# Low parts of the first expert's first layer made on DVE instead of POOL at the end of the attention

## The chip, the cores and the metric

The kernel runs on one core of a Trainium2 chip. The metric is the time of one execution on the device in microseconds (us). Five engines work in parallel, each through its own instructions in the order in which they were written: PE (matrix products), DVE (elementwise work and reductions), ACT (activations, copies, casts), POOL (a second, elementwise engine, which also issues gathers and scatters) and SP (issues most DMA transfers). They meet at semaphores: an instruction that needs a result of another engine waits at the head of its queue, and what is queued behind it waits too.

## The reference

Three stages follow one another on 4 x 544 tokens of width 512, all in float32.

```
# 1. attention: 8 heads of 64; 32 global and 512 local tokens, window 32
out_g = sm(scale * q_g @ k_all^T) @ v_all          # global tokens see all
s_ll  = where(|i - j| <= 32, scale * q_l @ k_l^T, -1e9)
out_l = sm(concat(scale * q_l @ k_g^T, s_ll)) @ concat(v_g, v_l)
# 2. mixture of experts: 8 experts, 512 -> 1024 -> 512
e = argmax(x @ w_gate), or the expert of the token before it where the local gate holds
x = softmax(x @ w_gate)[e] * (relu(x @ w1[e]) @ w2[e])
# 3. gated layer: 512 -> 1024, convolution over 3 tokens, sigmoid gate, 1024 -> 512
h = relu(x @ w_in);  out = (h * sigmoid(conv3(h))) @ w_out
```

## The kernel before

**Attention.** The work of a batch is cut into 8 units, and 32 units (n = 0 to 31) run one after the other in one loop that is written out as a software pipeline. Two units with the same 128 tokens (n even: heads 0 to 3, n odd: heads 4 to 7) share one output tile. For a unit, PE writes the scores `sp` (L259, L267, both units of a pair at once), DVE takes the row extremes `nm` (L275), ACT makes the exponentials `pr` (L278, four instructions), PE transposes them (`ptp`, L286), ACT copies them out (`pts`, L288), and two rounds later PE multiplies by V (`op`, L300). When both units of a pair are through, DVE normalises the tile (`rc`, `rr`, then `x`, L307 to L311). There is one PSUM buffer for `op`, so the first `op` of the next pair waits until `x` of the pair before has been read. SP stores `x` to `x_dram`; PE transposes it (`trx`, L319), DVE copies it out (`xt`, L321), and four such tiles give the router's logits (`lgp`, L334; `L`, L349).

**Routing and experts.** Tokens are sorted into slots of 128 of one expert each. The matrices of an expert are needed as a high and a low part, since each float32 product is made as three passes (high by high, high by low, low by high). `split_k` makes one piece: ACT casts the weights `ws` to the high part `wh` (L1026), then an elementwise engine subtracts, `wl = ws - wh` (L1027). For the first layer a piece is 128x1024, and there are four (k = 0 to 3).

**The end of the attention.** The first two slots are routed early, so that their expert's weights can be loaded and split while the attention still runs. `hook(n, 1)` is called at the end of round n: in rounds 28 to 31 it splits one piece of the first layer each (`SPLIT_W1`), and in rounds 30 and 31 it issues the loads of the second layer, which overwrite `ws` once the pieces there have been split. After the last round the rest of the pipeline is drained by hand: `op` of unit 30 and `x` of the last pair, the first matrix products of the expert (`hp`, L1090) between them, the second layer's splits on DVE (`SPLIT_W2`), the logits, and then the full routing (`phase_b`), whose DVE chain begins at `L` (L349) while PE goes on with slots 0 and 1 between its steps. Where it is said below that a row belongs to unit n, it is by this order.

Of the kernel before, what the change touches and what calls it, by code (L numbers as in the profile page):

```python
# [1566 lines left out]
def moe_kernel(ctx, tc, q_l, k_l, v_l, q_g, k_g, v_g, w_gate, w_local, w1, w2, w_in, conv_w, w_out, out):  # L1567
    nc = tc.nc
    outf = out.rearrange("b s d -> (b s) d")
    with tc.manual_schedule():  # L1570
# [37 lines left out]
        def hook(n, end):  # L1608
            if n + end > 20 and (end or todo.get("y") != "pe"):
                for _ in range(STEPS_A[end]):  # L1610
                    todo["y"] = next(ph, 0)
                    if todo["y"] == "es":
                        todo["load"] = True
                    if todo["y"] in (0, "pe"):
                        break
            if not end:
                return
            if n == N_Y:
                nc.sync.dma_start(y_dram[0:S, :], x_dram[0:S, :])
            if n == 25:  # L1620
                right.close()
                hl = ctx.enter_context(tc.tile_pool(name="w_hl", bufs=1, side="right"))
                st = moe_ctx.enter_context(tc.tile_pool(name="w_x", bufs=1, side="right"))
                W = Weights(nc, hl, st)
                m = todo["m"] = Moe(warm, tc, W, ident, x_dram, y_dram, rt, w1, w2, w_in.bitcast(I32),
                                    w_out.bitcast(I32))
            m = todo.get("m")
            if todo.pop("load", False):
                W = m.W
                todo["e0"] = m.reg(nc.sync, 0, 0, E - 1)  # L1630
                for a in (0, 2):
                    W.load_k(1, w1[bass.ds(todo["e0"], 1)], a, a + 2)
            if m and todo.get("y") == 0 and not m.xs and not m.xt:
                todo["g"] = n
                ca.close()
                todo["xp"] = xa.enter_context(tc.tile_pool(name="m_xa", bufs=1, side="right"))
                for s in range(NA):
                    m.xs[s] = m.gather(s, todo["xp"])
            if n - todo.get("g", n) == GATHER_T:
                m.hs0 = todo["xp"].tile([P, FF], F32, name="hs0")  # L1640
                m.xt[0] = m.hi_lo_t(m.xs.pop(0), NKC, "x", todo["xp"], at.ps)
            for k in SPLIT_W1.get(n, ()):
                m.W.split_k(1, m.W.s, k, nc.gpsimd)
            if n in (30, 31):
                for a in range(2):
                    k = 4 * (n - 30) + 2 * a
                    m.W.load_k(2, w2[bass.ds(todo["e0"], 1)], k, k + 2)
            if n == 32:
                cs.close()
                m.psh = moe_ctx.enter_context(tc.tile_pool(name="m_h", bufs=1, space=PSUM, side="right"))  # L1650
                todo["fill"] = m.fill()
            if n >= 32:
                for _ in range(TAIL[n - 32]):
                    next(todo["fill"])
                for k in SPLIT_W2.get(n, ()):
                    m.W.split_k(2, m.W.s, k, nc.vector)

        at = Attn(at_ctx, right, cs, tc, q_l, k_l, v_l, q_g, k_g, v_g, wcat, wz, ident, x_dram, L, late(), hook)
        at.run()
        at_ctx.close()  # L1660
        m, W, fill = todo["m"], todo["m"].W, todo["fill"]
# [61 lines left out]
```

## Time and profile before

| what | value |
|---|---|
| median of 3 runs | 648.47 us (646.09 to 649.37) |
| profiled execution | 645.35 us, of which 643.6 us are its span |
| PE busy | 604.7 us, 94% of the span |
| DVE busy | 418.8 us, 65% |
| ACT busy | 320.9 us, 50% |
| POOL busy | 174.7 us, 27% |

The span runs from the first to the last instruction, and all times of rows count from its start. Busy shares are means over stages of different kinds: in the attention all engines take turns in one pipeline, in the experts and the gated layer PE has nearly no gap.

### The profile page before, as it was taken

The page shows a single profiled execution, that of the slowest core. Times are in us where ns is not written, and L with a number is a line of the kernel's source. Part 1 is how long each engine was busy: PE and PEld are TensorE (multiplying, and loading weights), DVE is VectorE, ACT ScalarE, POOL GpSimd, SP SyncE. Part 2 cuts the span into 40 slices and gives each one's busy share as a digit, 9 for nine tenths or more (in the row PEclk, how much of TensorE's full clock was granted, in tenths as well). Part 3 has the DMA queues.
Part 4 walks back from the last instruction along what each step waited for, and adds up shares of the span by engine and source line. Part 5 has one row for each costly group of instructions (what it writes and reads, how often), then busy time and mean ns, then how long its engine had stood idle before and what let it go on. Part 6 is the DMA issues. An engine that isn't in the chain of part 4 may idle for free. (4 is left out here: it accounts for less than half of the span.)

```text
span 643.6 us, 15270 instructions
## 1 busy us (share of the span) xinstructions
PE 604.7 (94%) x5898; PEld 508.0 (79%) x5898; DVE 418.8 (65%) x874; ACT 320.9 (50%) x629; POOL 174.7 (27%) x226
## 2 busy tenths in 40 slices
PE   8888898888999999999999999987999999999997
PEld 7666676665778888888888888857998898898986
DVE  7877577958836676875778677586893393393340
ACT  4754555573225546352454634664874374373331
POOL 7664810070212232423222251000042042300200
PEclk9999999999999999999999999997999999999999
DMA  9999668652158454953545494023101201000001
GB/s 226 217 244 236 177 142 209 240 168 75 55 201 314 140 182 171 344 207 132 211 143 184 145 347 157 16 86 88 31 20 49 68 16 50 34 1 34 34 34 49
DMA packets 60089, 88.12 MB, mean 137 GB/s; under 512 B 25710, under 2 KB 34182, under 8 KB 59976
## 3 DMA queue, kind: packets, MB, share of 16 engines
q1 hardware_dynamic: 56488, 76.83, 38.3%
q0 software_dynamic: 3520, 10.23, 4.6%
q8 instruction: 48, 0.79, 0.5%
q14 instruction: 33, 0.27, 0.1%
HBM read 125.87 MB, written 15.79 MB: 220 GB/s over the span
## 5 line engine op out<-in xcount | busy, mean ns | idle before, releaser
L1433 DVE SCALAR_TENSOR_TENSOR fc<-f_hp,cw,fc 128x544 f32<-128x544 f32 (+2 forms) x66 | 51.4, 778 | 71.5 <-ACT fc L1431 70.0
L1027 DVE TENSOR_TENSOR wl<-ws,wh 128x512 fp32r<-128x512 f32 (+1 forms) x92 | 71.8, 848 | 5.3 <-ACT wh L1026 5.2
L1106 PE MATMUL yp<-wh,gh 128*128 128x512 f32 x176 | 71.0, 404 | 1.1 <-ACTq L1277 0.9
L1106 PE MATMUL yp<-wl,gh 128*128 128x512 f32 x176 | 69.0, 392 | 0.7 <-DVEq L1277 0.7
L1106 PE MATMUL yp<-wh,gl 128*128 128x512 f32 x176 | 69.1, 393 | 0.0
L1026 ACT CAST wh<-ws 128x512 fp32r<-128x512 f32 (+1 forms) x96 | 66.1, 779 | 0.0
L1255 ACT ACTIVATE hs<-hp 128x512 f32<-128x512 f32 x44 | 24.3, 595 | 74.2 <-PE hp L1090 74.1
L1090 PE MATMUL hp<-wh,xh 128*128 128x512 f32 x176 | 58.6, 405 | 0.7 <-ACT xh L1079 0.7
L1090 PE MATMUL hp<-wl,xh 128*128 128x512 f32 x176 | 56.2, 392 | 0.0
L1090 PE MATMUL hp<-wh,xl 128*128 128x512 f32 x176 | 56.0, 391 | 0.0
L1491 PE MATMUL f<-wh,fh 128*128 128x512 f32 (+1 forms) x144 | 55.5, 385 | 0.0
L1491 PE MATMUL f<-wl,fh 128*128 128x512 f32 (+1 forms) x144 | 55.0, 382 | 0.0
L1491 PE MATMUL f<-wh,fl 128*128 128x512 f32 (+1 forms) x144 | 55.0, 382 | 0.0
L1063 POOL DMA_INDIRECT y_dram<-ys,sidx x22 | 24.6, 1118 | 105.7 <-ACT ys L1259 88.9
L1083 DVE TENSOR_TENSOR gl<-hlp,gh 128x512 fp32r<-128x512 f32 x44 | 28.4, 686 | 32.4 <-ACT gh L1079 32.3
L278 ACT ACTIVATE pr<-sp,nm 128x128 f32<-128x128 f32 x128 | 36.6, 376 | 25.7 <-DVE nm L275 25.7
L999 POOL TENSOR_TENSOR wf<-wf,fx 128x512 int32<-128x512 int32 x16 | 20.8, 1303 | 100.9 <-DVE fx L998 100.9
L1259 ACT COPY ys<-yp 128x512 f32<-128x512 f32 x22 | 12.9, 587 | 61.2 <-PE yp L1106 56.5
L1051 POOL DMA_INDIRECT xs<-x_dram,gidx x22 | 27.5, 1249 | 45.5 <-ACT pr L278 34.0
L1106 PEld LDWEIGHTS yp<-wh,gh 128*128 128x128 f32 x176 | 33.1, 188 | 7.7 <-ACTq L1277 1.1
L1090 PEld LDWEIGHTS hp<-wl,xh 128*128 128x128 f32 x176 | 32.9, 188 | 7.8 <-DVE wl L1027 0.9
L1106 PEld LDWEIGHTS yp<-wh,gl 128*128 128x128 f32 x176 | 33.0, 188 | 7.6 <-DVE gl L1083 0.6
(357 smaller groups left out, 1492.5 us busy)
## 6 DMA issues: line engine op xcount, KB each, us to landing
ws<-in_moe_w_dram SPq DMA_DIRECT2D x42, 2048.0 KB
fx<-y_dram SPq DMA_DIRECT2D x17, 256.0 KB
raw<-in_k_l_dram SPq DMA_DIRECT2D x16, 256.0 KB
x_dram<-x SPq DMA_DIRECT2D x16, 256.0 KB
fx<-in_moe_w_in_dram SPq DMA_DIRECT2D x8, 512.0 KB
fx<-in_moe_w_out_dram SPq DMA_DIRECT2D x8, 512.0 KB
out_dram<-fy SPq DMA_DIRECT2D x16, 256.0 KB
VA<-in_v_l_dram SPq DMA_DIRECT2D x20, 192.0 KB
```

Source lines behind the costliest of these rows:

```text
L278: nc.scalar.activation(pr[:, hp, :], sp[:, hp, :], AF.Exp, bias=nm[:, hp:hp + 1], scale=-1.0)
L999: nc.gpsimd.tensor_tensor(a, a, lo, ALU.add)
L1026: (cp.tensor_copy if cp else self.nc.scalar.copy)(h, src[n][:, k, :])
L1027: eng.tensor_tensor(l, src[n][:, k, :], h.bitcast(F32), ALU.subtract)
L1051: self.nc.gpsimd.indirect_dma_start(out=xs, out_offset=None, in_=self.x_dram[0:n, :], in_offset=bass.IndirectOffsetOnAxis(ap=self.rt.gidx[ ...
L1063: self.nc.gpsimd.indirect_dma_start(out=self.y_dram[:, :], out_offset=bass.IndirectOffsetOnAxis(ap=self.rt.sidx[:, s:s + 1], axis=0), in_= ...
L1083: self.nc.vector.tensor_tensor(hl[1][:, a:a + 4], t, hl[0][:, a:a + 4].bitcast(F32), ALU.subtract)
L1090: self.nc.tensor.matmul(hp[c], a[:, k, :], b[:, 512 * c:512 * c + 512], start=k == 0 and m == 0, stop=k == NKC - 1 and m == 2)
L1106: self.nc.tensor.matmul(yp, a[:, k, :], b, start=k == 0 and m == 0, stop=k == NFC - 1 and m == 2)
L1255: self.nc.scalar.activation(hs[:, 512 * c:512 * c + 512], hp[c], AF.Relu)
L1433: nc.vector.scalar_tensor_tensor(c[:, a:b], hp[:, a + t:b + t], self.cw[:, t, f:f + 1], c[:, a:b], ALU.mult, ALU.add)
L1491: self.nc.tensor.matmul(yp[:, cs], x[:, c], w[:, cs], start=f == 0 and n == 0, stop=f == NFC - 1 and n == 2)
```

## The change

The subtraction that makes `wl` of the four first-layer pieces in rounds 28 to 31 is given to DVE. The cast on ACT, the places in the program and the data are the same. On PE, ACT and SP the order of the instructions is the same.

```diff
             for k in SPLIT_W1.get(n, ()):
-                m.W.split_k(1, m.W.s, k, nc.gpsimd)
+                m.W.split_k(1, m.W.s, k, nc.vector)
```

On POOL, the four subtractions stood behind the gather of the first two slots' tokens (`xs`) and ahead of the branch that begins the next expert's split; this is the difference there, from before to after.

```order
 L1051 DMA xs<-x_dram,gidx 128x512 x2
-L1027 TENSOR_TENSOR wl_0_2725<-ws_2723,wh_0_2724 128x1024
-L1027 TENSOR_TENSOR wl_1_2727<-ws_2723,wh_1_2726 128x1024
-L1027 TENSOR_TENSOR wl_2_2729<-ws_2723,wh_2_2728 128x1024
-L1027 TENSOR_TENSOR wl_3_2731<-ws_2723,wh_3_2730 128x1024
 L1270 TENSOR_LOAD esi
```

POOL's queue now goes from that gather to the branch with nothing between.

On DVE, this is the queue before in rounds 30 and 31 and the beginning of the drain: `nm_3210` and `nm_3264` are the row extremes of units 30 and 31, `xt_3229` the copy of the tile of units 26 and 27, `rc`, `rr` and `x_3291` the normalisation of units 28 and 29, `xt_3320` the copy of the global tokens' tile.

```order
L275 TENSOR_REDUCE nm_3210<-sp_3168 128x4
L321 COPY xt_3229<-trx_3224 128x512
L275 TENSOR_REDUCE nm_3264<-sp_3169 128x4
L307 TENSOR_SCALAR rc_3287<-op_3231 128x8
L309 RECIPROCAL rr_3289<-rc_3287 128x8
L311 TENSOR_TENSOR x_3291<-op_3231,rr_3289 128x512
L321 COPY xt_3320<-trx_3315 128x512
```

And the same stretch of DVE's queue after the change:

```order
L1027 TENSOR_TENSOR wl1_1_2727<-ws2_2723,wh1_1_2726 128x1024
L275 TENSOR_REDUCE nm_3210<-sp_3168 128x4
L321 COPY xt_3229<-trx_3224 128x512
L1027 TENSOR_TENSOR wl1_2_2729<-ws2_2723,wh1_2_2728 128x1024
L275 TENSOR_REDUCE nm_3264<-sp_3169 128x4
L307 TENSOR_SCALAR rc_3287<-op_3231 128x8
L309 RECIPROCAL rr_3289<-rc_3287 128x8
L311 TENSOR_TENSOR x_3291<-op_3231,rr_3289 128x512
L1027 TENSOR_TENSOR wl1_3_2731<-ws2_2723,wh1_3_2730 128x1024
L321 COPY xt_3320<-trx_3315 128x512
```

Piece 1 now stands ahead of the row extremes of unit 30, piece 2 ahead of those of unit 31, and piece 3 between the last pair but one's `x` and the copy of the global tokens' tile. Each waits there for ACT's cast of the same piece.

Piece 0 stands one round earlier on DVE, right ahead of the row extremes of unit 29 (`nm_3087`) and the normalisation of units 26 and 27:

```order
L1027 TENSOR_TENSOR wl1_0_2725<-ws2_2723,wh1_0_2724 128x1024
L275 TENSOR_REDUCE nm_3087<-sp_2978 128x4
L307 TENSOR_SCALAR rc_3117<-op_3042 128x8
L309 RECIPROCAL rr_3119<-rc_3117 128x8
L311 TENSOR_TENSOR x_3121<-op_3042,rr_3119 128x512
```

Before, this stretch began with `nm_3087`; the rest is as it was.

## Rows read from the trace of the kernel before

**Rows 1.** The page: busy time, share of the span and instructions of each engine.
```profile
PE 604.7 (94%) x5898; PEld 508.0 (79%) x5898; DVE 418.8 (65%) x874; ACT 320.9 (50%) x629; POOL 174.7 (27%) x226
```

**Rows 2.** PE by stretches: us, busy, granted clock (1.00 is full), DMA share, GB/s.
```profile
160.00:200.00 40.00, 37.76 (x196) 1.00 0.47 163
200.00:420.00 220.00, 219.96 (x1070) 1.00 0.52 186
434.00:437.00 3.00, 0.03 (x1) 1.00 0.05 14
437.00:444.00 7.00, 5.73 (x25) 0.51 0.55 145
```

**Rows 3.** Timeline of POOL: start, us, engine, line, operation, [idle before <- what ended it].
```profile
134.28 2.37 POOL L1027 TENSOR_TENSOR wl<-ws,wh 128x1024 fp32r<-128x1024 f32 x1 [1.44 <-ACT wh L1026]
...
140.32 4.87 POOL L1027 TENSOR_TENSOR wl<-ws,wh 128x1024 fp32r<-128x1024 f32 x2 [0.74 <-ACT wh L1026]
```

**Rows 4.** Timeline of PE and of SP's queue around the drain.
```profile
141.36 0.22 PE L300 MATMUL op<-VC,pts 128*32 128x65 f32 x1 [1.34 <-ACT pr L278]
...
146.29 1.06 PE L334 MATMUL lgp<-xt,wcat 128*32 128x128 f32 x8
147.28 0.50 PE L1090 MATMUL hp<-wh,xh 128*128 128x512 f32 x1
...
142.71 2.88 SPq L1022 DMA_DIRECT2D ws<-in_moe_w_dram  x2
```

**Rows 5.** Timeline of ACT, rounds 28 to 31.
```profile
133.15 1.05 ACT L1026 CAST wh<-ws 128x1024 fp32r<-128x1024 f32 x1
134.10 1.14 ACT L278 ACTIVATE pr<-sp,nm 128x128 f32<-128x128 f32 x4
...
136.05 1.09 ACT L1026 CAST wh<-ws 128x1024 fp32r<-128x1024 f32 x1
137.67 1.14 ACT L278 ACTIVATE pr<-sp,nm 128x128 f32<-128x128 f32 x4 [0.53 <-DVE nm L275]
...
139.16 1.08 ACT L1026 CAST wh<-ws 128x1024 fp32r<-128x1024 f32 x1
...
140.58 1.19 ACT L278 ACTIVATE pr<-sp,nm 128x128 f32<-128x128 f32 x4
141.59 1.11 ACT L1026 CAST wh<-ws 128x1024 fp32r<-128x1024 f32 x1
```

**Rows 6.** Timeline of DVE, rounds 29 to 31 and the drain.
```profile
133.22 0.68 DVE L275 TENSOR_REDUCE nm<-sp 128x4 f32<-128x512 f32 x1
...
136.90 0.68 DVE L275 TENSOR_REDUCE nm<-sp 128x4 f32<-128x512 f32 x1
137.50 0.68 DVE L321 COPY xt<-trx 128x512 f32<-128x512 f32 x1
138.09 0.68 DVE L275 TENSOR_REDUCE nm<-sp 128x4 f32<-128x512 f32 x1
140.08 0.17 DVE L307 TENSOR_SCALAR rc<-op 128x8 f32<-128x8 f32 x1 [1.31 <-PE op L300]
...
140.52 0.69 DVE L311 TENSOR_TENSOR x<-op,rr 128x512 f32<-128x512 f32 x1
142.65 0.69 DVE L321 COPY xt<-trx 128x512 f32<-128x512 f32 x1 [1.44 <-PE trx L319]
```

**Rows 7.** DVE's own `wl` by shape, 190 to 300 us: busy us, mean ns.
```profile
L1027 DVE TENSOR_TENSOR wl<-ws,wh 128x1024 fp32r<-128x1024 f32 x12 | 13.9, 1220 | 0.3 <-ACT wh L1026 0.3
```

**Rows 8.** Timeline of DVE and PE at the last logits.
```profile
149.48 1.90 DVE L1027 TENSOR_TENSOR wl<-ws,wh 128x512 fp32r<-128x512 f32 x3 [0.80 <-ACT wh L1026]
151.30 0.68 DVE L321 COPY xt<-trx 128x512 f32<-128x512 f32 x1
...
152.03 0.41 PE L334 MATMUL lgp<-xt,wcat 128*32 128x128 f32 x2 [1.14 <-DVE xt L321]
```

**Rows 9.** Waits of PE after the attention: total us, times, longest.
```profile
PE f L1414 <- PEq L1179: 4.2, 1, 4.2
```

## The prediction

> **What bounds the kernel now.** I read the busy shares first, then PE by stretches, then the timelines of the five engines where the four pieces are made. PE is busy 94% of the span, POOL 27% [rows 1], so a lighter POOL is worth nothing as such; the question is whether POOL's pieces are on PE's way, and what DVE's would be. From 200 to 420 us PE has no gap (219.96 of 220 us), and from 160 to 200 us it has 2.24 us [rows 2]. So a delay that reaches PE at the attention's end is carried through the experts to the end, except for what those gaps give back.
>
> The pieces are made from 134.28 to 145.19 us, the last two back to back (4.87 us for two, so 2.4 us each) [rows 3]. The expert's matrix products that read the last piece begin at 147.28 us [rows 4], 2.1 us after it is done. No wait of PE in this stretch is for POOL. The one wait of PE here is 1.34 us, to 141.36, at the first `op` of unit 30 [rows 4]. The label names ACT's exponentials, but those of unit 31 end later and those of unit 30 long before. What fits is the single `op` buffer: DVE's `x` of units 28 and 29 ends at 140.52 + 0.69 = 141.21 [rows 6], 0.15 us ahead of the `op`. So the chain of the attention's end already runs through DVE here: `rc` and `x` wait for PE's `op` of unit 29, and PE waits for `x`.
>
> **The change part by part.** It takes four subtractions off POOL, where they delay nobody (gain 0), and adds four to DVE. DVE has a row for the same shape: 1.22 us [rows 7], half of POOL's. The row of the next instruction begins 0.08 us before the end of the one ahead (`nm` of unit 30 ends at 137.58, `xt` begins at 137.50) [rows 6], so one costs 1.14 us in a queue. A hand-over between DVE and ACT takes 0.09 us (`nm` of unit 30 ends at 137.58, `pr` begins at 137.67) [rows 5, 6]. The four 1.14 us are not the point. Each piece stands ahead of the next unit's `nm` or of `x`, and waits for ACT's cast; ACT makes the cast in the same round, and its next exponentials wait for the `nm` behind the piece. POOL did this waiting with nothing behind it. On DVE it makes a ring: cast, piece, `nm`, exponentials, next cast. I follow it piece by piece; "later" is against the row.
>
> *Piece 0.* The cast ends at 133.15 + 1.05 = 134.20 [rows 5]. The piece begins at 134.29, and `nm` of unit 29 at 135.43 instead of 133.22 [rows 6]. Its exponentials begin 0.68 + 0.09 later, at 136.20 instead of 134.10 [rows 5]: **+2.10 us**. PE had written the scores, so nothing else is waited for.
>
> *Piece 1.* Everything behind on ACT moves by 2.10: the cast of piece 1 ends at 136.05 + 1.09 + 2.10 = 139.24. The piece begins at 139.33, `nm` of unit 30 at 140.47 instead of 136.90, the exponentials at 141.24 instead of 137.67: 3.57 us later, so **+1.47 us** more. This is less than 2.1 because `nm` of unit 30 was late already.
>
> *Piece 2.* The cast ends at 139.16 + 1.08 + 3.57 = 143.81, the piece begins at 143.90, `nm` of unit 31 at 145.04, and `rc` of units 28 and 29 right behind it at 145.72 instead of 140.08 [rows 6]: 5.64 us later, so **+2.07 us** more. PE's `op` of unit 29 waits only for copies behind the exponentials of unit 30; it ended where PE's 1.34 us wait began, at 140.02, and with 3.57 us more at 143.59, ahead of `rc`. `x` ends at 146.85, and the `op` of unit 30 begins at 147.00 instead of 141.36 [rows 4]. Here 5.64 us reach PE.
>
> *Piece 3.* Exponentials of unit 31 begin at 145.72 + 0.09 = 145.81 instead of 140.58 (5.23 later), the cast ends at 141.59 + 1.11 + 5.23 = 147.93, and the piece lies from 148.02 to 149.24. Behind it stands the copy of the global tokens' tile, which PE's shift alone would bring to 142.65 + 5.64 = 148.29 [rows 6]; it begins at 149.16, 0.87 us late, and is done at 149.85. Its reader on PE, the first logits at 146.29 + 5.64 = 151.93 [rows 4], has 2 us to spare, and the products with piece 3 at 147.28 + 5.64 = 152.92 have 3.7. So piece 3 costs 0, hidden behind PE's `op`, transposes and first products; without that cover it would cost the 0.87.
>
> *Transfers.* The second layer's loads wait for the pieces, because they overwrite `ws`. The last two stand at 142.71 on SP [rows 4], released by POOL's pieces 2 and 3; they would go behind the store of `x` (146.85) and behind piece 3 (149.24). Their casts stand behind the first products on PE, which also move by 5.64; the later one loses some 149.24 - 145.19 = 4.1 us and so keeps all its lead. Cost 0.
>
> Behind this point the queues keep their order, and all that follows (the last `x`, the logits, the routing chain on DVE, PE's products between) hangs on PE or DVE, both 5.64 us late. That a piece at the head of DVE's queue holds up PE is to be seen already: before the last logits DVE waits 0.80 us for ACT's cast, then makes three pieces, then the copy at 151.30, and PE stands still 1.14 us for that copy [rows 8]. Nothing in the change moves this wait; it goes along.
>
> **Sum.** 2.10 + 1.47 + 2.07 + 0 = 5.64 us, taken as 5.6. Against its own execution this is 645.35 + 5.6 = 651.0. The median of the runs shown is 648.47, 3.1 above that execution, and the prediction stands against the median: 648.47 + 5.6 = **654.1 us**, 0.87% slower. Bounds: if the later gaps of PE (2.24 us from 160 to 200 [rows 2]) gave all they have, 3.4 us remain: 651.9. Above, see the clock.
>
> **The rivals.** *PE's clock falls as well.* In the forecast PE stands still from 143.59 to 147.00, 3.4 us, after another thin stretch. In this trace the longest wait of PE is 4.2 us [rows 9]; the clock was at 1.00 while PE stood from 434 to 437 us, and 0.51, the 1.2 GHz level, from 437 to 444 [rows 2]. The 1.34 us wait has no such fall. 3.4 lies nearer to 4.2 than to 1.3, but the gap ends sooner, and it comes behind some work. Price: at most half of 7 us, so 3.4 us more: 657.5. The Trainium skill ("TensorE: Matmul & The Clock Gate", section "Why this matters for your kernels") tells one to avoid idle gaps of TensorE between bursts of matrix products, because an idle gap that is long enough takes it back to half rate. This speaks against the change, and by that rule the sum would be the 9.0 us of this rival; the trace agrees for the 4.2 us wait, and shows nothing for a gap of 3.4.
>
> *Part is given back.* DVE's and ACT's chains in the routing have idle time that could absorb some; what speaks against it is that the routing begins with logits that come late themselves. Price: 3.4 us, 651.9.
>
> *No loss: the piece finds its cast done.* If ACT made its casts before DVE came to them, the pieces would fall into DVE's idle time, 1.31 and 1.44 us ahead of `rc` and of `xt` [rows 6]. For piece 0 this would take a cast that ends 1.0 us sooner (134.20, where DVE is free for `nm` at 133.22). Then 4 x 1.14 us meet that idle time, the second layer's loads go a little sooner, and at best the 1.14 us wait [rows 8] is gone: 647.3 to 648.5. The rows speak against it: ACT is full where the casts stand, and POOL waited for casts too (1.44 and 0.74 us [rows 3]).
>
> **How the numbers follow.** Forecast 0.66; clock 0.14; part given back 0.08; no loss 0.12. A change of 0.5%, 3.2 us, is about what a measurement of this kernel can tell from none: slower are the first two whole and 0.06 of the third, 0.86; of the last, 0.02 might be read as faster; its rest and that of the third are the same, 0.12. The range leaves out the no-loss case alone: 650.8 to 657.8, with part given back (651.9) and the clock (657.5) inside it, and 1.1 us below the former for the spread of the runs (646.09 to 649.37). The chance that it holds is a little over 8 in 10.
>
> **What would show it.** `nm` of unit 29 begins at about 135.4, of unit 30 at 140.5, of unit 31 at 145.0, each right behind a piece on DVE that waited for ACT; PE has gaps ahead of the transposes of unit 30 and a gap of some 3.4 us ahead of the `op` of unit 30, at 147.0; the first row of the routing chain comes 5 to 6 us later than before; POOL has no subtraction of this kind. A granted clock under 1.00 between 143 and 155 us would speak for the first rival; a routing that ends less than 5 us late, for the second. I am wrong if the pieces start without waiting for ACT, or if PE does not wait for `x` there.

## The result and the profile after

The changed kernel takes 655.32 us (median of 7 executions, 652.36 to 657.78) against 648.47 us (7 executions, 645.44 to 651.54) of the kernel before in the same comparison: a ratio of 1.011, 95% interval 1.0082 to 1.0139. The forecast was 654.1 us. The profiled execution took 652.36 us, of which 650.6 us are its span: 7.0 us more in either than before (645.35 and 643.6).

The page's busy row of the kernel after answers to [rows 1]:

```profile
PE 606.0 (93%) x5898; PEld 509.6 (78%) x5898; DVE 422.2 (65%) x878; ACT 321.2 (49%) x629; POOL 167.6 (26%) x222
```

DVE has four instructions and 3.4 us more, POOL four fewer and 7.1 us less. Neither number says where 7 us come from. The timeline of DVE does (start, us, engine, line, operation, [idle before <- what ended it]); it answers to [rows 6]:

```profile
133.95 1.23 DVE L1027 TENSOR_TENSOR wl<-ws,wh 128x1024 fp32r<-128x1024 f32 x1 [1.33 <-ACT wh L1026]
135.09 0.69 DVE L275 TENSOR_REDUCE nm<-sp 128x4 f32<-128x512 f32 x1
...
138.96 1.23 DVE L1027 TENSOR_TENSOR wl<-ws,wh 128x1024 fp32r<-128x1024 f32 x1 [0.25 <-ACT wh L1026]
140.10 0.68 DVE L275 TENSOR_REDUCE nm<-sp 128x4 f32<-128x512 f32 x1
...
143.47 1.23 DVE L1027 TENSOR_TENSOR wl<-ws,wh 128x1024 fp32r<-128x1024 f32 x1 [2.09 <-ACT wh L1026]
144.61 0.69 DVE L275 TENSOR_REDUCE nm<-sp 128x4 f32<-128x512 f32 x1
...
145.64 0.69 DVE L311 TENSOR_TENSOR x<-op,rr 128x512 f32<-128x512 f32 x1
147.44 1.23 DVE L1027 TENSOR_TENSOR wl<-ws,wh 128x1024 fp32r<-128x1024 f32 x1 [1.11 <-ACT wh L1026]
148.66 0.69 DVE L321 COPY xt<-trx 128x512 f32<-128x512 f32 x1
...
160.99 0.20 DVE L349 COPY L<-r_t 128x36 f32<-128x36 f32 x1 [0.69 <-PE r_t L346]
```

Every piece waits for ACT, and every `nm` stands right behind a piece. ACT in turn waits for the `nm`, which [rows 5] shows only once and for 0.53 us:

```profile
132.87 1.05 ACT L1026 CAST wh<-ws 128x1024 fp32r<-128x1024 f32 x1
135.87 1.14 ACT L278 ACTIVATE pr<-sp,nm 128x128 f32<-128x128 f32 x4 [1.95 <-DVE rc L307]
137.83 1.09 ACT L1026 CAST wh<-ws 128x1024 fp32r<-128x1024 f32 x1
140.88 1.14 ACT L278 ACTIVATE pr<-sp,nm 128x128 f32<-128x128 f32 x4 [1.95 <-DVE nm L275]
142.35 1.08 ACT L1026 CAST wh<-ws 128x1024 fp32r<-128x1024 f32 x1
145.33 1.14 ACT L278 ACTIVATE pr<-sp,nm 128x128 f32<-128x128 f32 x4 [1.41 <-DVE nm L275]
```

(The label `rc` at 135.87 is the event that came last by the profile; `nm` ended 0.09 us before.) PE, with [rows 4] before it, has gaps behind both:

```profile
137.54 0.66 PE L286 MATMUL ptp<-ident,pr 128*128 128x128 f32 x4 [1.43 <-ACT pts L288]
...
141.30 1.10 PE L286 MATMUL ptp<-ident,pr 128*128 128x128 f32 x4 [2.06 <-ACT pr L278]
...
146.48 0.29 PE L300 MATMUL op<-VC,pts 128*32 128x65 f32 x1 [3.27 <-ACT pr L278]
...
158.88 1.06 PE L334 MATMUL lgp<-xt,wcat 128*32 128x128 f32 x8 [1.15 <-DVE xt L321]
```

At the 3.27 us gap the label names ACT again, but DVE's `x` of units 28 and 29 ends at 145.64 + 0.69 = 146.33 us, 0.15 us ahead of the `op` at 146.48, as it did before: PE waits for `x`.

PE by stretches (us, busy of PE, PEld, DVE, ACT and POOL, granted clock, DMA share, GB/s) shows a second loss:

```profile
133.00:143.40 10.40, 6.57 (x232) 4.95 (x230) 6.42 (x12) 6.49 (x15) 0.00 (x0) 1.00 0.33 89
143.40:150.20 6.80, 3.72 (x43) 3.39 (x44) 4.71 (x7) 3.29 (x9) 0.00 (x0) 0.50 0.72 230
150.20:161.00 10.80, 9.60 (x100) 6.95 (x99) 7.69 (x17) 4.63 (x9) 0.00 (x0) 1.00 0.21 72
```

Before, the clock was 1.00 all through here. Now it falls to the 1.2 GHz level 0.2 us after the 3.27 us gap began (143.2 us), behind 10.4 us in which PE was busy for 63%.

**Where the 7 us are.** Three marks cut both executions: the start of piece 0's cast on ACT, the start of unit 30's `op` on PE, and the first row of the routing chain (L349). Before, L349 stood here:

```profile
154.14 0.20 DVE L349 COPY L<-r_t 128x36 f32<-128x36 f32 x1 [0.69 <-PE r_t L346]
```

| stretch | before | after | difference |
|---|---|---|---|
| start to cast of piece 0 | 133.15 | 132.87 | -0.28 |
| cast of piece 0 to `op` of unit 30 (the ring) | 8.21 | 13.61 | +5.40 |
| `op` of unit 30 to L349 (the drain) | 12.78 | 14.51 | +1.73 |
| L349 to the end of the span | 489.4 | 489.6 | +0.2 |

The theory is that the ring of cast, piece, `nm`, exponentials and next cast makes the 5.4 us, and the clock in the drain the other 1.7. Its rivals: the work alone does it (four subtractions in a full DVE queue), the wait alone does it, or the 1.7 us of the drain come from something other than the clock.

### The profile page after: what moved, and what is told of

It is laid out like the page before. It is cut to its first block, busy times and chain, and to the rows that moved or that the text cites. A ratio compares the mean times of both kernels' runs of the same rounds, so it can differ in the third digit from the quotient of the medians.

```text
span 650.6 us, 15271 instructions
## 1 busy us (share of the span) xinstructions
PE 606.0 (93%) x5898; PEld 509.6 (78%) x5898; DVE 422.2 (65%) x878; ACT 321.2 (49%) x629; POOL 167.6 (26%) x222
## 5 line engine op out<-in xcount | busy, mean ns | idle before, releaser
L1027 DVE TENSOR_TENSOR wl<-ws,wh 128x512 fp32r<-128x512 f32 (+1 forms) x96 | 76.7, 863 | 10.0 <-ACT wh L1026 10.0
L1063 POOL DMA_INDIRECT y_dram<-ys,sidx x22 | 26.8, 1219 | 126.9 <-ACT ys L1259 110.0
```

What stands on the lines that cost most here:

```text
L1027: eng.tensor_tensor(l, src[n][:, k, :], h.bitcast(F32), ALU.subtract)
L1063: self.nc.gpsimd.indirect_dma_start(out=self.y_dram[:, :], out_offset=bass.IndirectOffsetOnAxis(ap=self.rt.sidx[:, s:s + 1], axis=0), in_= ...
```

## The experiments

All kernels were timed beside the kernel before (medians of 6 to 12 executions; that of before was 647.4 to 648.5 us). The table gives three of the four stretches of each profiled execution, and for how long of the drain the clock was at the lower level (from the mean granted clock of the drain). The stretch ahead of the cast, which isn't part of the theory, took between 132.0 and 139.5 us in these executions, and each median holds other falls of the clock too; so an effect of one or two microseconds is read from the stretches and not from the medians.

| kernel | median, us | ratio (95%) | ring | drain | rest | low clock in the drain |
|---|---|---|---|---|---|---|
| before | | | 8.21 | 12.78 | 489.4 | 0 |
| after | 655.3 | 1.011 (1.008-1.014) | 13.61 | 14.51 | 489.6 | 3.7 |
| e9_again | 656.2 | 1.012 (1.007-1.017) | 13.61 | 14.93 | 491.0 | 4.7 |
| e1_lag | 651.2 | 1.004 (1.001-1.007) | 9.35 | 14.36 | 490.4 | 3.4 |
| e2_wait | 653.5 | 1.011 (1.008-1.015) | 10.39 | 12.78 | 491.2 | 0 |
| e2b_wait | 652.7 | 1.006 (1.003-1.009) | 10.38 | 15.43 | 490.7 | 5.8 |
| e4_late | 652.6 | 1.006 (1.003-1.009) | 10.12 | 15.43 | 490.5 | 5.7 |
| e5_last | 647.9 | 1.002 (0.999-1.005) | 8.20 | 14.34 | 489.4 | 3.4 |
| e3_fill | 656.8 | 1.016 (1.012-1.020) | 16.2 | 12.8 | 491.3 | 0 |
| e3b_fill | 655.8 | 1.010 (1.006-1.013) | 13.60 | 12.77 | 492.2 | 0 |
| e6_w2pool | 651.5 | 1.005 (1.001-1.008) | 8.21 | 13.14 | 494.7 | 3.4 |
| e7_shift | 649.9 | 1.001 (0.998-1.004) | 8.21 | 12.77 | 491.3 | 0 |
| e8_shift64 | 651.7 | 1.006 (1.003-1.010) | 8.22 | 14.36 | 493.7 | 3.4 |

**The work without the wait (e1_lag).** Each subtraction goes to DVE one round behind its cast, and the last of the second layer's loads moves behind the last piece. The main part of the edit, against the kernel before (the `lag` switch of `split_k` and the loads are left out):

```diff
+            for low in todo.pop("low", ()):
+                low()
             for k in SPLIT_W1.get(n, ()):
-                m.W.split_k(1, m.W.s, k, nc.gpsimd)
+                todo["low"] = (m.W.split_k(1, m.W.s, k, nc.vector, lag=True),)
```

> All four subtractions on DVE, each put one round behind its cast (the last load of the second layer moves behind the last piece, with SP's order the same). Theory of the ring (the wait for ACT's cast at the head of DVE's queue makes most of the loss): DVE finds every cast done; by the rows of before, nm of unit 30 begins 1.14 us late behind piece 0, the op of unit 30 begins 1.1 us late, pieces 2 and 3 are hidden: 1.1 us over before, the row of L349 22.1 us after the first cast's start (21.0 before, 28.1 in the changed kernel), no fall of the clock at this place. Rival (DVE's added work itself is the loss): 4 x 1.14 = 4.6 us over before.

No piece waits any more on DVE, and the ring shrinks from +5.40 to +1.14 us (9.35 - 8.21), one subtraction. The expectation that the clock would not fall here failed: it was low for 3.4 us of the drain, so that the first row of the routing chain came 23.7 us after the cast and not 22.1. The median is 3.8 us above before; at equal clock (below) it is 1.1 (standard error 0.5). From DVE's timeline of this kernel:

```profile
139.19 1.22 DVE L1027 TENSOR_TENSOR wl<-ws,wh 128x1024 fp32r<-128x1024 f32 x1
140.32 0.68 DVE L275 TENSOR_REDUCE nm<-sp 128x4 f32<-128x512 f32 x1
140.92 0.68 DVE L321 COPY xt<-trx 128x512 f32<-128x512 f32 x1
141.52 1.22 DVE L1027 TENSOR_TENSOR wl<-ws,wh 128x1024 fp32r<-128x1024 f32 x1
```

**The wait without the work (e2_wait, e2b_wait).** The subtractions stay on POOL; DVE copies one column of each fresh `wh` at the same place, in e2_wait into a new tile (`probe`) of 4 bytes a partition, in e2b_wait into a scratch tile that exists (`warm`). The edit of e2_wait, without the line that makes the tile:

```diff
             for k in SPLIT_W1.get(n, ()):
                 m.W.split_k(1, m.W.s, k, nc.gpsimd)
+                nc.vector.tensor_copy(probe, m.W.t[1][k][0][:, 0:1].bitcast(F32))
```

> The kernel before, with the subtractions on POOL, and one copy of a single column of the freshly cast piece on DVE at each of the four places where the change puts the subtraction: the wait without the work. Theory of the ring: nm of unit 29 1.2 us late, exponentials 1.1; nm of unit 30 at 1.5, nm of unit 31 and rc of units 28 and 29 at 2.5: the op of unit 30 begins 2.5 us late, 2.5 us over before (wait and work don't add up: 1.1 alone for the work, 2.5 alone for the wait, 5.4 together in the trace). Rival (the work is the loss): 4 copies of about 0.1 us, within 0.5 us of before.

> The wait without the work again, the column now written into a tile that was there already, so that no tile behind it moves. Theory of the ring: from the first cast's start to the op of unit 30 10.4 us, as with the new tile (8.2 before, 13.6 in the changed kernel), the products of the experts at 392 ns as before, and some 2.2 us over before where the clock falls as often. Rival (the excess of 4 us of the run with the new tile belongs to the wait): again 6 us over before.

The ring is +2.18 and +2.17 us. DVE's timeline of e2_wait shows `nm` held up by a copy that costs next to nothing itself:

```profile
135.53 0.15 DVE L1645 COPY probe<-wh 128x1 f32<-128x1 f32 x1 [0.92 <-ACT wh L1026]
135.60 0.68 DVE L275 TENSOR_REDUCE nm<-sp 128x4 f32<-128x512 f32 x1
```

The wait alone gives 2.2 and the work alone 1.1. Together they give 5.4, 2.1 more than their sum: in a ring the subtraction itself delays the next cast, which the next subtraction waits for. e2_wait's median is 6.1 us above before, much more than its ring; its products in the experts took 395 ns where those of before took 391, and those of e2b_wait, without the new tile, 391 again (below).

**Two pieces, and the last alone (e4_late, e5_last).** Against the kernel before, for e4_late:

```diff
-                m.W.split_k(1, m.W.s, k, nc.gpsimd)
+                m.W.split_k(1, m.W.s, k, nc.vector if k > 1 else nc.gpsimd)
```

(e5_last: `k > 2`.)

> Pieces 2 and 3 on DVE, 0 and 1 on POOL. Theory of the ring: piece 2 alone puts off nm of unit 31 and the rc behind it by 2.07 us, piece 3 nothing: 10.3 us from the first cast's start to the op of unit 30 (8.2 before), 2.1 us over before at the same clock. Rival (each piece costs a quarter of the whole 5.4): 2.7 us, or (only the first two count): 0.

> Only piece 3 on DVE, pieces 0 to 2 on POOL. Theory of the ring: piece 3 stands behind x of units 28 and 29 with no nm behind it, so it is hidden: the op of unit 30 and L349 within 0.2 us of before, time the same. Rival (every piece costs its work): 1.1 us. A third way (every piece costs a quarter of the loss): 1.4 us or more.

Pieces 2 and 3 alone cost 1.91 us in the ring, just what the third step costs in the whole change (below). Piece 3 alone costs nothing there (8.20), and none in the drain: 14.34 us with 3.4 us of low clock, where e8_shift64, with no piece on DVE and as much low clock, has 14.36. The time is that of before within the interval.

**The clock (e3_fill, e3b_fill).** The changed kernel, with products of zeros on PE whose result nobody reads, ahead of the transposes of unit 30 and ahead of its `op`: 14 and 24 in e3_fill, 7 and 10 in e3b_fill. Each has two rows in the profile. The edit of e3b_fill against the changed kernel, in part:

```diff
+                self.fill_pe(wt, 7)
                 pts[n - 1] = self.pt(units[n - 1], pr.pop(n - 1))
 ...
+        self.fill_pe(wt, 10)
         pv_norm(N - 2)
```

> The changed kernel with products of zeros on PE that nobody reads: 14 ahead of the transposes of unit 30 (some 1.7 us in a gap of 2.1) and 24 ahead of the op of unit 30 (some 2.9 us in a gap of 3.3). Theory of the clock (the fall to 0.50 from about 143.6 to 150.4 us costs 1.7 us, the time by which the stretch from the op of unit 30 to the last trx is longer than before): no fall between 135 and 160 us, that stretch 6.7 us as before instead of 8.5, and 1.7 us less than the changed kernel, so 5.4 over before. Rival (PE waits for others there anyhow, the fall costs nothing): the clock stays up and the time is that of the changed kernel, 7.1 over before.

> The changed kernel with fewer products of zeros on PE, 7 ahead of the transposes of unit 30 and 10 ahead of the op of unit 30, since one took 0.24 us and not 0.12 in the first try (1.7 and 2.4 us now, in gaps of 2.1 and 3.3). Theory of the clock: no fall between the first cast and the logits, 13.6 us from the first cast's start to the op of unit 30 as in the changed kernel, 12.8 us from there to L349 as before (14.5 in the changed kernel), and 1.5 to 3 us less than the changed kernel. Rival: the fall costs nothing, the time is that of the changed kernel.

In e3_fill the fillers took longer than the gaps (3.39 and 5.62 us for gaps of 2.06 and 3.27) and pushed the `op` out themselves. In e3b_fill they fitted: PE's timeline has 0.83 us left of the 3.27.

```profile
142.81 1.83 PE L230 MATMUL wf<-wz 128*128 128x128 f32 x14
144.94 1.10 PE L290 MATMUL ptp<-ident,pr 128*128 128x128 f32 x4 [0.31 <-ACT pr L282]
146.79 2.50 PE L230 MATMUL wf<-wz 128*128 128x128 f32 x20
150.12 0.22 PE L304 MATMUL op<-VC,pts 128*32 128x65 f32 x1 [0.83 <-ACT pr L282]
```

The ring is the same to 0.01 us (13.60), the clock stays up, and the drain has its old length:

```profile
136.50:163.00 26.50, 22.57 (x409) 17.89 (x409) 18.96 (x37) 14.56 (x31) 0.00 (x0) 1.00 0.39 122
```

So the ring owes nothing to the clock, and the 1.73 us of the drain are the clock's. The drains of the other kernels agree. These are before, after and e2b_wait:

```profile
141.36:154.14 12.78, 11.59 (x141) 8.79 (x142) 8.37 (x18) 6.67 (x13) 3.73 (x2) 1.00 0.55 180
146.48:160.99 14.51, 13.31 (x141) 10.31 (x142) 9.59 (x19) 6.25 (x11) 0.00 (x0) 0.87 0.36 110
144.75:160.18 15.43, 14.23 (x141) 10.96 (x142) 8.52 (x18) 6.24 (x11) 2.82 (x2) 0.81 0.36 116
```

PE is idle for 1.2 us in each; what grows is its busy time, by 1.72 and 2.64 us. Over all kernels but e6_w2pool, whose edit lies in the drain, the drain is 12.8 us without low clock, 14.3 to 14.4 with 3.4 us, 14.5 with 3.7, 14.9 with 4.7 and 15.4 with 5.7 or 5.8: 0.46 us more for each microsecond at the lower level.

But the kernel as a whole is no faster than the changed one (1.0097 against 1.011), where 1.5 to 3 us less were expected. Its rest took 492.2 us, 2.7 more than before. In its profiled execution the clock fell later instead, 183 us into the span, and some 1.5 us of the 2.7 lie in the experts, up to their last product; e9_again, with a like fall there, has 1.6 more than before. The other 1.2 us came behind the experts, and their cause is open.

**The changed kernel again (e9_again).**

> The changed kernel once more, unchanged, for how far its parts repeat. The ring should repeat to 0.1 us (13.6 us from the first cast's start to the op of unit 30). The fall of the clock: if PE's thin stretch there brings it about, it is there again, with 14.3 to 15.5 us from the op of unit 30 to L349; if it was chance, it may be gone, with 12.8. Time within 0.3% of the first, 655.3.

The ring repeats to 0.01 us (150.88 - 137.27 = 13.61), and the median within 0.2%. The clock falls again, 2.2 us ahead of the `op` where it was 3.1 in the first execution, so that more of the low level lies in the drain, which is 0.42 us longer:

```profile
148.80:155.60 6.80, 4.71 (x45) 4.19 (x46) 3.78 (x7) 3.76 (x9) 0.00 (x0) 0.50 0.74 242
```

**A tile that nobody needs (e7_shift, e8_shift64).** The kernel before, with one more tile of 4 or of 64 bytes a partition, which shifts the tiles allocated after it.

```diff
+        probe = cp.tile([P, 1], F32, name="probe")
+        nc.vector.memset(probe, 0.0)
```

> The kernel before with one more tile of 4 bytes in each partition ahead of the others, set to zero at the start and not used. If the new tile's 4 bytes, by moving all tiles behind it, made the products slower in the run of the wait (396 ns for 392 in the experts): 396 ns again, 8.2 us from the first cast to the op of unit 30, and 2.5 to 4 us over before. If they did not: time and products as before.

> Control to the shift: the kernel before with an unused tile of 64 bytes instead of 4 in each partition. If what made the products slower is where tiles begin within 64 bytes: 392 ns in the experts as before, 489.5 us from L349 to the end (491.2 with 4 bytes), time as before. If any shift or the added instruction does it: 396 ns again.

One shape of the experts' products, from 210 to 410 us (busy us, mean ns of one), in e8_shift64 and in e6_w2pool, which has no such tile and the number of before:

```profile
L1090 PE MATMUL hp<-wl,xh 128*128 128x512 f32 x128 | 40.4, 396 | 0.0
```

```profile
L1090 PE MATMUL hp<-wl,xh 128*128 128x512 f32 x132 | 41.0, 392 | 0.0
```

Both sizes slow the products by 1% (e7_shift and e2_wait have 397 ns for this shape; all ten kernels without the tile have 392). It isn't the added `memset`, which e2_wait lacks. The first way of e8_shift64's expectation, in which only the place within 64 bytes counts, came out false. From L349 to the last product of the experts the three kernels with the tile took 282.9 to 283.0 us, where before took 278.9: 4 us. In e2_wait and e7_shift about 2.2 us of that come back behind the experts, in e8_shift64 nothing does. By its median e7_shift can't be told from before (0.998 to 1.004), where 2.5 to 4 us were expected; at equal clock (below) it is 2.4 us above before and e8_shift64 5.0 (standard errors 0.5). Why a tile that nobody uses has such an effect stays open. The changed kernel, with 392, is not touched by it.

**Another wait on ACT in the same stretch (e6_w2pool).** In the kernel before, five of the second layer's subtractions (k = 3 to 7) go from DVE to POOL, to take away DVE's 0.80 us wait for ACT's cast and with it PE's 1.14 us [rows 8].

```diff
-                    m.W.split_k(2, m.W.s, k, nc.vector)
+                    m.W.split_k(2, m.W.s, k, nc.gpsimd if k > 2 else nc.vector)
```

> The kernel before with the opposite exchange a little later: the subtractions of the second layer's pieces 3 to 7 go from DVE to POOL, where nothing is queued behind them, so that the copy of the last tile before the logits no longer stands behind pieces 3 to 5 on DVE. If the queue order is what counts: PE's wait of 1.1 us for that copy is gone, and from the op of unit 30 to L349 it takes 11.6 to 11.8 us instead of 12.8; 1.0 to 1.2 us less than before, too little for the times to show. Rival (POOL's 1.2 us for a piece makes the products of slot 0 wait): no gain, and waits of PE for POOL behind L349.

PE's wait is gone: the drain is 13.14 us with the clock low for 3.4 us in it, where e5_last with as much has 14.34, so 1.2 us shorter. What came instead stands in the routing chain, in the timelines of POOL and DVE:

```profile
151.98 6.24 POOL L1027 TENSOR_TENSOR wl<-ws,wh 128x512 fp32r<-128x512 f32 x5 [5.97 <-ACT wh L1026]
```

```profile
155.60 0.23 DVE L683 TENSOR_REDUCE r_m<-L 128x9 f32<-128x72 f32 x1
155.88 1.15 DVE L685 TENSOR_SCALAR r_rel<-L 128x9 f32<-128x9 f32 x1
156.94 1.37 DVE L688 TENSOR_TENSOR r_eq<-L,r_m 128x72 f32<-128x72 f32 x1
158.23 0.15 DVE L689 TENSOR_TENSOR r_rel<-r_rel,c_keep 128x1 f32<-128x1 f32 x1
```

Before, the rows of L685 and L688 took 0.17 and 0.23 us. They end where POOL's subtractions end (each 6.24 / 5 = 1.25 us; the last at 158.22). The Trainium skill ("SBUF — State Buffer", section "SBUF: two separate sides") says that DVE and GpSimd (POOL) share a pair of ports that one instruction holds to its end, and that a DVE instruction with two inputs from SBUF, or in a mode that takes both ports, has to wait for it. The trace agrees for L688, which has two inputs; L685 has one, and in which mode it ran no row shows. The two lost 2.1 us. PE then waits 2.7 us at L707 (0.50 before), the clock falls again behind that, and the rest is 5.2 us longer. So the rival's no gain came true, by another way than the products that it named.

## Why the prediction was right

*The ring, step by step.* Against the start of piece 0's cast, the exponentials of unit 29 begin 3.00 us later instead of 0.95, +2.05 (forecast +2.10); those of unit 30 8.01 instead of 4.52, so +1.44 more (+1.47); the `op` of unit 30 13.61 instead of 8.21, so +1.91 more (+2.07). The sum is 5.40 against 5.64. What is missing lies in hand-overs: pieces 0 to 2 begin 0.03 to 0.04 us behind the ends of their casts (143.47 against 142.35 + 1.08 for piece 2), where 0.09 was taken, and `x` begins 1.03 us after `nm` of unit 31, where 1.12 was taken (the prediction counted `nm` there with its whole 0.68 us, though it had found that the next row begins 0.08 us before its end). The starts of `nm` (135.09, 140.10, 144.61) were forecast at 135.4, 140.5 and 145.0 on the axis of before, of which 0.28 us is the earlier start of the cast.

*Piece 3.* It delays the copy of the global tokens' tile by 6.29 us against the cast, where PE's shift is 5.40: 0.89 us of its own, forecast 0.87, and hidden as forecast; e5_last shows 0.00 for the piece alone.

*Part given back.* No: from L349 to the end after is 0.2 us longer than before. What PE loses at the attention's end is carried to the end.

*No loss.* No: every piece waited, and e2b_wait shows that the place in the queue costs 2.2 us without the work.

*The clock.* This rival was given 0.14 and came in both profiled executions of the changed kernel, as well as the ring. Its price was put at half of 7 us, 3.4 us, and the drain shows 1.73 and 2.15 us. The half is near what the drains show (0.46); what the price left out is that the clock fell while PE waited for `x` anyway, so that 3.1 and 2.2 us of the 6.8 at the lower level cost nothing there. And the fall was tied to the gap of 3.4 us, with the thin stretch ahead of it only named, while in the first execution it began 0.2 us into that gap. Nor is a gap of this length needed. Six of the profiled kernels have the 1.34 us wait of [rows 4] within 0.01 us (before, e1_lag, e5_last, e6_w2pool, e7_shift, e8_shift64), and in four of them the clock was low for 3.4 us in the drain. In the three of these whose drain no edit shortens that is 1.6 us of time (14.34 against 12.78). The profiled execution of before had none, so the comparison of these two traces makes the clock's share look larger than a mean over executions would. That the median came out 6.85 us higher, and not 5.6, is by the stretches the ring's 5.4 and part of a clock price whose size varies from execution to execution. The forecast of 654.1 took the ring alone and set the clock apart as a rival; that it lies within 1.2 us of the median is owed to the ring, which was worked out, and to the small share of the clock, which is luck: the sum had it at nothing, and its rival at 3.4 us.

How far this split holds can be read from the timed executions. A straight line through 189 of them, by the mean clock of each and with a level for each kernel, gives 0.41 us (standard error 0.03) for each microsecond at the lower clock, and what each kernel is above before at equal clock. For the experiments this agrees with their rings: 1.1 us for e1_lag (ring 1.14), 2.0 for e2b_wait (2.17), 2.6 for e4_late (1.91) and 0.2 for e5_last (0), each with a standard error of 0.5; e3b_fill has 6.6 (0.7), its ring of 5.39 and the 1.2 us behind the experts. The changed kernel is 3.9 us (0.6) above before by its first seven executions and 4.6 (0.7) by e9_again's; 2.8 and 3.6 us go with a lower mean clock (0.985 and 0.983 against 0.990). The traces put its ring at 5.4. That the line gives this ring less and the clock more stays open; and so the times alone do not show that wait and work together cost more than their sum of some 3.1 us, which rests on the stretches, equal to 0.01 us in two profiles.

## What to carry to other kernels

Before moving an instruction from an idle engine to a busy one, ask what it waits for and what is queued behind it: an engine with nothing behind its wait gives that waiting away for nothing, while here two engines that waited for each other in the same round turned 1.1 us of work and 2.2 us of waiting into 5.4 us. If the work has to move, put it a round behind what it waits for (e1_lag kept four fifths of the loss off the ring). Of a product-bound kernel with falls of the clock, compare stretches between marks, since the total of one execution moves by more than many edits are worth.

## What the runs showed of the hardware

- DVE makes a 128x1024 subtraction in 1.23 us, POOL in 2.4; the faster engine was the wrong one.
- One unused tile slowed the experts' matrix products from 392 to 396 or 397 ns, with 4 and with 64 bytes, and the experts by 4 us; the cause is open.
- In the drain, where PE is idle for only 1.2 us of 12.8, each microsecond at the lower clock cost 0.46 us.
- Two DVE instructions of 0.2 us took 1.15 and 1.37 us while POOL subtracted in SBUF (e6_w2pool).
- The clock of a stretch differed between executions of like kernels: with a 1.34 or 1.35 us wait of PE, it was low for 3.4 us in the drain in four profiles and not at all in two.
